# A hand-written order of tasks on five engines: the start of a modulated attention and gated block in another order, the values of tile 3 first

## The chip, the cores and the metric

The kernel runs on one core of a Trainium2 chip. The metric is the device time of one execution in microseconds. Beside the runs that only give a time there is one profiled execution, whose trace gives the start and length of every instruction.

## What is computed

The input `x` has 2048 rows of 512 (bf16). A vector `c` gives six rows of modulation. The first half is a linear attention of 32 heads of 16, whose features are two softmaxes; the second half is a gated block with 1376 hidden columns.

```python
mod = (silu(c) @ w_mod).reshape(1, 6, 1, -1)        # sa, ca, ga, sb, cb, gb
h = layernorm(x) * (1 + ca) + sa
q, k, v = split_heads(h @ wqkv)                      # 32 heads of 16
phi(t) = concat(softmax(t @ w_phi), softmax(-(t @ w_phi)))
kv = sum_s phi(k)_s v_s ;  z = sum_s phi(k)_s
o = phi(q) kv / (phi(q) z + 1e-6)
x = x + ga * (o @ wo)
h = layernorm(x) * (1 + cb) + sb
return x + gb * ((sigmoid(h @ w_gate) * (h @ w_up)) @ w_down)
```

## The kernel before

The 2048 rows are 16 tiles of 128. Everything is cut into 1230 named tasks, each a few instructions on one engine, and a text, `ORDER` (from line 39), lists them all. `arrange` (line 137 on) goes through the text word by word. It gives each task its engine (the first one the task allows, or the one behind `@`: A is ScalarE, D is VectorE, P is GpSimd) and gives each buffer a slot at its first use; a slot goes back to the end of its free list when the last user in the text is past. `emit` then issues the tasks in that order. So the text sets three things: the order of each engine's queue, the engine of some tasks, and which buffer a task takes over from which. An engine works its queue strictly in order; a task whose input is missing holds up all that stands behind it on the same engine. PSUM is eight banks, handed on in this way.

The names that are needed here, with their lines:

- `ld_*` (lines 533 to 563): loads, issued by SyncE onto one queue. `ld_x0b` is tiles 2 and 3 of x, `ld_x0a` tiles 0 and 1, `ld_wk0`/`ld_wk1` the key weights, `ld_wm00a` to `ld_wm01b` four quarters of the modulation weights (256 KB each, line 542), `ld_x3a` tiles 12 to 15 of x (512 KB, line 537), `ld_wv0` all value weights (512 KB, line 551), `ld_wmga` the modulation weights for ga (512 KB, line 555). `wqT*` are transposing loads of the query weights (line 669).
- `warm0`, `warm1_0` to `warm1_11` (line 600): matmuls on zeros, which nothing reads.
- `c1`, `c2`, `c3`: silu of c. `modc1.0`, `modc1.1` (line 630): the products that give sa and ca, the first for columns j = 0, 1, the second for j = 2, 3; `modc1c0`, `modc1c1` copy them out.
- `tpw*`, `wTc*`, `fold1*`, `foldc1*` (lines 661 to 685): key weights transposed, multiplied with w_phi, copied; `fold0*` the same for the queries.
- `st1_t` (lines 702, 703): statistics of tile t on VectorE. `rs1_g` (line 709 on ScalarE, 712 on GpSimd): the inverse deviation of group g; groups are tile 0, tile 1, tiles 2 and 3, and so on in pairs. `nmr1_g` (718), `xn1_t` (727 ScalarE, 729 VectorE, 731 GpSimd): the normalised tile.
- `tphgj` (line 744): TensorE transposes column block j of group g into a bank. `hm1_gj` (751 ScalarE, 753 VectorE): modulation of that block, out of the bank into `h1T`.
- `Kt`, `Vt`, `Qt` (lines 817, 821, 871): four matmuls of 512 columns each. For tiles 0 to 7 K, and for tiles 0 to 3 V, are halves: `K3a` takes j = 0, 1, `K3b` j = 2, 3. `K3a` needs `hm1_20`, `hm1_21` and the folded key weights; `V3a` needs `hm1_20`, `hm1_21` and `ld_wv0`.
- `et`, `nt`, `rt`, `phit` (776 to 798): exponentials on ScalarE, sums and reciprocals mainly on VectorE, the features. `vat` copies V out on ScalarE, `kvt` accumulates phi(k) v.
- `num`, `rd`, `u`, `out`, `x1`, `st2`, `xn2`, `mod`: the rest of the attention and the second norm. `gk.f`, `uk.f`, `tgk.f`, `hmk.f`, `yt.f` (lines 447, 457, 468, 485): the gated block of chunk k; chunk 0 is tile 0, chunk 1 is tile 1, then come 2, 4, 4 and 4 tiles. `g1.2` is the first gate product of the second chunk.

A load also waits for an earlier load: eight semaphores go round among the transfers.

## Time and profile before

| | us |
|---|---|
| three runs | 202.90, 204.34, 409.55 (median 204.34) |
| profiled execution | 203.25 |
| its span, first to last instruction | 201.3 |
| TensorE busy | 193.6 |
| VectorE busy | 160.0 |
| ScalarE busy | 104.9 |
| GpSimd busy | 103.9 |

How to read the profile. PE is TensorE's matmuls, PEld its weight loads, DVE is VectorE, ACT ScalarE, POOL GpSimd, SP SyncE. `L817` is line 817 of the kernel. A row of the timeline gives start, length, engine, line, operation, what it writes and reads, and how many were merged (`x6`); in square brackets stands the idle time before it and what ended it. A row of the waits gives who waited for whom, the total, how often and the longest. A row that ends in `KB, 5.0` is an issued transfer with its size and its time from issue to landing.

### The profile page before, as it was taken

How to read it: one execution, taken by the hardware profiler on the slowest of the kernel's cores; microseconds unless marked ns; L12 is line 12 of the kernel's file. 1: busy time of each engine (PE TensorE's matmuls, PEld its weight loads, DVE VectorE, ACT ScalarE, POOL GpSimd, SP SyncE). 2: the span in 40 equal slices, each digit the busy share in tenths (PEclk: the TensorE clock that was granted, in tenths of full speed). 3: DMA queues.
4: the chain of work that ended last, by engine and by line, in shares of the span. 5: the costliest groups of instructions: out<-in, count | busy, mean ns of one | idle time of the engine just before them, and what ended most of it. 6: DMA issues, size and time to landing. Idle time of an engine off the chain costs nothing.

```text
span 201.3 us, 4128 instructions
## 1 busy us (share of the span) xinstructions
PE 193.6 (96%) x1447; PEld 106.1 (53%) x1471; DVE 160.0 (79%) x376; ACT 104.9 (52%) x250; POOL 103.9 (52%) x146
## 2 busy tenths in 40 slices
PE   7889999999999999999999999999999999999993
PEld 2555665455565777668744444444444444444442
DVE  3999999999999999997997796875969662326632
ACT  2899999999978974486621215312112420334100
POOL 4889978887899998876660166130030332000000
PEclk9999999999999999999999999999999999999999
DMA  5999956729964883455573334442113031000011
GB/s 163 336 292 236 295 204 126 113 62 268 396 248 78 133 111 68 85 34 105 104 80 80 70 62 102 84 110 56 25 25 74 2 78 55 26 8 26 28 55 55
DMA packets 49453, 22.94 MB, mean 114 GB/s; under 512 B 38065, under 2 KB 47634, under 8 KB 49426
## 3 DMA queue, kind: packets, MB, share of 16 engines
q1 hardware_dynamic: 48896, 22.59, 48.8%
q8 instruction: 13, 0.21, 0.4%
q14 instruction: 14, 0.11, 0.2%
q10 hardware_dynamic: 530, 0.02, 0.1%
HBM read 11.58 MB, written 2.10 MB: 68 GB/s over the span
## 4 chain that ended last, share of the span: by engine, by line
PE 64%; DVE 26%; issue 5%; ACT 2%; DMA 1%; DVEq 0%
PE y_ps L485 19%; PE u_ps L447 18%; PE g_ps L447 18%; DVE ks L780 6%; PE a_ps L356 5%; DVE st L702 5%; DVE qks L780 3%; DVE phi L787 3%; DVE kr L798 2%; PE num L326 2%; DVE h1T L753 2%; DMA x_sb<-in_A_x_dram 1%; DVE mv L703 1%; PE g_ps L449 1%; DVE nmr L718 1%
## 5 line engine op out<-in xcount | busy, mean ns | idle before, releaser
L457 ACT ACTIVATE tg<-g_ps 128x512 bf16<-128x512 f32 (+5 forms) x66 | 28.7, 455 | 66.6 <-PE g_ps L447 39.7
L468 DVE SCALAR_TENSOR_TENSOR wmod_sb<-tg,u_ps 128x512 bf16<-128x512 bf16 (+4 forms) x63 | 30.2, 491 | 18.1 <-ACT tg L457 11.5
L485 PE MATMUL y_ps<-wd_sb,wmod_sb 128*128 128x512 bf16 (+4 forms) x180 | 44.2, 366 | 0.2
L447 PEld LDWEIGHTS <-wg_sb 128*128 128x128 bf16 (+1 forms) x252 | 21.9, 99 | 16.1 <-issue 0.2
L447 PEld LDWEIGHTS <-wu_sb 128*128 128x128 bf16 (+1 forms) x252 | 21.7, 99 | 15.9 <-issue 0.2
L784 POOL TENSOR_TENSOR qphi<-qe,qks 128x512 bf16<-128x512 bf16 x24 | 25.2, 1066 | 3.9 <-DMA pT<-qphi 1.6
L485 PEld LDWEIGHTS <-wmod_sb 128*128 128x128 bf16 (+1 forms) x187 | 17.1, 98 | 16.0 <-issue 0.6
L447 PE MATMUL u_ps<-wT_sb,wu_sb 128*128 128x512 bf16 (+2 forms) x124 | 23.8, 322 | 0.1
L447 PE MATMUL g_ps<-wT_sb,wg_sb 128*128 128x512 bf16 (+2 forms) x122 | 23.0, 321 | 0.2
L447 PE MATMUL g_ps<-wqk_sb,wg_sb 128*128 128x128 bf16 (+4 forms) x127 | 19.9, 286 | 0.1
L447 PE MATMUL u_ps<-wqk_sb,wu_sb 128*128 128x128 bf16 (+4 forms) x127 | 19.8, 286 | 0.1
L492 DVE TENSOR_TENSOR ot<-y_ps,x 128x512 bf16<-128x512 f32 (+2 forms) x17 | 11.1, 654 | 10.4 <-PE y_ps L485 10.3
L780 DVE TENSOR_REDUCE ks<-e 128x64 f32<-128x1024 bf16 (+2 forms) x22 | 19.2, 901 | 0.0
L780 DVE TENSOR_REDUCE qks<-qe 128x64 bf16<-128x1024 bf16 x16 | 19.1, 1202 | 0.0
L376 POOL TENSOR_SCALAR ve<-mv 128x2 f32<-128x2 f32 (+1 forms) x8 | 1.8, 225 | 33.3 <-DVE mv L366 33.2
L776 ACT ACTIVATE e<-k_ps 128x512 bf16<-128x512 f32 (+2 forms) x44 | 18.2, 519 | 0.0
L776 ACT ACTIVATE qe<-q_ps 128x512 bf16<-128x512 f32 x32 | 17.0, 611 | 0.8 <-POOL phi L787 0.5
L817 PE MATMUL k_ps<-wqk_f,h1T 128*128 128x512 bf16 x61 | 16.0, 379 | 0.1
L787 POOL TENSOR_TENSOR phi<-e,kr 128x1024 bf16<-128x1024 bf16 (+2 forms) x10 | 14.8, 1484 | 2.6 <-DVE phi L787 1.2
L356 PE MATMUL a_ps<-wo_sb,oT 128*128 128x512 bf16 x60 | 15.9, 379 | 0.2
L871 PE MATMUL q_ps<-wqk_f,h1T 128*128 128x512 bf16 x61 | 15.7, 379 | 0.1
L821 PE MATMUL v_ps<-wv_sb,h1T 128*128 128x512 bf16 x61 | 15.4, 379 | 0.1
(132 smaller groups left out, 305.6 us busy)
## 6 DMA issues: line engine op xcount, KB each, us to landing
out_dram<-ot SPq DMA_DIRECT2D x15, 128.0 KB, 1.7
x_sb<-in_A_x_dram SPq DMA_DIRECT2D x6, 256.0 KB, 4.7
wmod_sb<-in_w_mod_dram SPq DMA_DIRECT2D x1, 1536.0 KB, 7.0
wu_sb<-in_B_w_up_dram SPq DMA_DIRECT2D x1, 1376.0 KB, 11.5
wg_sb<-in_B_w_gate_dram SPq DMA_DIRECT2D x1, 1376.0 KB, 11.9
wd_sb<-in_B_w_down_dram SPq DMA_DIRECT2D x1, 1280.0 KB, 8.5
wmod_sb<-in_w_mod_dram SPq DMA_DIRECT2D x4, 256.0 KB, 6.1
wqk_sb<-in_A_wqkv_dram SPq DMA_DIRECT2D x2, 256.0 KB, 4.4
```

The costliest lines, as they stand in the source:

```text
L356: pe.matmul(ap_[:], lhsT=oT[:, j, :], rhs=wo_sb[:, j, :], start=(j == 0), stop=(j == KT - 1))
L447: pe.matmul(ps[:fsz, 0:n], lhsT=w[:, j, ft * P:ft * P + fsz], rhs=h[:, j, 0:n], start=(j == 0), stop=(j == KT - 1))
L457: G.add(f"tg{k}.{ft}", {"ACT": 0.13 + n * 0.00083}, lambda e, tg=tg, g_ps=g_ps, fsz=fsz, n=n: act.activation(tg[:fsz, 0:n], g_ps[:fsz, 0:n ...
L468: dve.scalar_tensor_tensor(hm_all[:fsz, hm[k].slot, ft, 0:n], tg[:fsz, 0:n], 1.0, u_ps[:fsz, 0:n], op0=ALU.add, op1=ALU.mult)
L485: mm = pe.matmul(y[:, 0:c1 - c0], lhsT=hm_all[:fsz, hm[k].slot, ft, tl * P:(tl + 1) * P], rhs=wd_sb[:fsz, ft, c0:c1], start=(ft == 0), sto ...
L776: act.activation(ee[:, a:b, s].rearrange("p g f h -> p g (f h)"), kp[:, a * 64:b * 64].rearrange("p (g n) -> p g n", n=64), ACT.Exp, scale ...
L780: dve.tensor_reduce(ks[:, a:b].rearrange("p g s h -> p (g s) h"), ee[:, a:b].rearrange("p g s f h -> p (g s) h f"), axis=AX.X, op=ALU.add)
L784: engine(e).tensor_tensor(ph[:].rearrange("p (g s f h) -> p g s f h", s=2, f=DH, h=4)[:, :, s], ee[:, :, s], ks[:, :, 1 - s].unsqueeze(2). ...
L787: engine(e).tensor_tensor(ph[:, a * P:b * P].rearrange("p (g f h) -> p g f h", f=DH, h=4), ee[:, a:b].rearrange("p g s f h -> p (g s) f h" ...
L817: pe.matmul(kp[:], lhsT=h1T[:, j, t * P:(t + 1) * P], rhs=wqk_f[:, j, D:2 * D], start=(j == 0), stop=(j == KT - 1))
L821: pe.matmul(vp[:], lhsT=h1T[:, j, t * P:(t + 1) * P], rhs=wv_sb[:, j, :], start=(j == 0), stop=(j == KT - 1))
L871: pe.matmul(qp[:], lhsT=h1T[:, j, t * P:(t + 1) * P], rhs=wqk_f[:, j, 0:D], start=(j == 0), stop=(j == KT - 1))
```

## The change

Only the text `ORDER` changes, and in it only the first 582 words, up to `g1.2`; the 648 words from there on are the same in both, and so are all tasks and what they need from each other. SyncE's queue keeps its order up to `ld_wo`, its 23rd entry. Three tasks go to another engine: `rs1_0` from GpSimd to ScalarE, `rs1_1` and `xn1_3` from ScalarE to GpSimd.

On TensorE the queue around the beginning is, before: ... `modc1.0 warm1_10 tph11 tph12 warm1_11 tph01 tph23 fold13 tph00 modc1.1 K3a tph02 tph03 K0a tph41 tph40 K2a fold01 tph42 K2b K0b K3b tph32 tph30 tph31 tph33 K1a K1b V0a` ..., and after: ... `tph21 warm1_9 tph20 modc1.0 warm1_10 tph22 warm1_11 tph03 fold13 tph11 tph23 modc1.1 tph10 V3a tph12 K3a tph13 fold01 tph40 tph41 tph42 V3b K0a tph30 tph33 tph32 K3b tph31 K0b tph43 K2a K2b K1a V1a K1b V2a` ... . On VectorE, `st1_0` and `xn1_0` come five and six places earlier, `hm1_10` five later, `st1_9` behind `hm1_40` and not ahead of it. On ScalarE the queue behind `modc1c0` is now `hm1_01 hm1_00 hm1_20 hm1_11 hm1_21 foldc13 hm1_22 hm1_12 hm1_03 foldc01 hm1_13 hm1_42 va3`. Later on, most tasks move by zero to five places on their engine, a few by more (`V6` 17 earlier, `V12` 12, `Q5` 10).

The beginning of the diff, where this stands:

```diff
-wdz warm0 c1 warm1_0 warm1_1 warm1_2 warm1_3 warm1_4 warm1_5 warm1_6 warm1_7 ld_x0b pmem ld_x0a ld_wk0 tpw1 tpw0 bd c2 mask4 st1_3 st1_2 st1_1 ld_x1b warm1_8
-rs1_2 rs1_1 nmr1_2 ld_wk1 xn1_3@A c3 wTc1 ld_x1a warm1_9 xn1_2 tph22 tph20 tpw2 tph21 wTc0 nmr1_1 st1_6 wTc2 xn1_1 tph13 ld_wm00b st1_0 tph10 tpw3 wTc3 fold10
-rs1_0@P fold12 st1_7 foldc10 ld_wm00a foldc12 fold11 modc1.0 rs1_4@P ld_x2b warm1_10 foldc11 modc1c0 st1_5 tph11 tph12 ld_wm01b warm1_11 st1_4 rs1_3@P
-hm1_20@A xn1_0 hm1_10 hm1_11@A hm1_21@A tph01 tph23 fold13 tph00 nmr1_4 xn1_6 xn1_7 ld_wm01a st1_11 hm1_01@A foldc13 st1_10 modc1.1 K3a modc1c1@D ld_x2a
-hm1_00@A tph02 hm1_23 rs1_6@P hm1_13@A hm1_02 nmr1_3 st1_9 st1_8 xn1_5 tph03 K0a tph41 hm1_03@A tph40 xn1_4 K2a hm1_22@A hm1_12@A hm1_41@A hm1_40 wqT1 nmr1_6
-ld_x3a st1_15 fold01 foldc01 tph42 K2b hm1_42@A K0b K3b e0.0 ld_wv0 tph32 tph30 tph31 wqT3 tph33 rs1_5@P nmr1_5 K1a hm1_32 xn1_11 hm1_30@A st1_14 n0.0 st1_12
-xn1_10 xn1_9 K1b e2.0 e3.0 rs1_8@P V0a wqT2 xn1_8 hm1_31@A tph43 V2a V2b nmr1_8 xn1_15 xn1_14 ld_wmga wqT0 V3a V3b va3 V0b fold03 V1a modca.0 modca.1 hm1_33
-tph50 V1b e1.0 K5a n2.0 r0.0@A modcac hm1_50 n3.0 hm1_43@A foldc03 xT1_11 fold02 fold00 foldc02 phi0.0 tph52 foldc00 xT1_10 va2 va1 n1.0 va0 K5b K4a r3.0
-st1_13 tph53 hm1_63@P hm1_60@P K4b hm1_62@P Q0 hm1_53@A tph51 Q1 ld_wmm2 tph82 hm1_51@A r2.0@A Q2 r1.0 phi3.0@D phi1.0@D hm1_82@A qe0.0 Q4 modc2.0 phi2.0@D
...
+wdz warm0 c1 mask4 pmem ld_x0b warm1_0 warm1_1 warm1_2 warm1_3 warm1_4 st1_3 warm1_5 ld_x0a st1_2 bd ld_wk0 c2 tpw0 rs1_2 st1_0 rs1_0 tpw1 wTc0 ld_x1b st1_1
+rs1_1@P warm1_6 nmr1_2 ld_wk1 wTc1 warm1_7 tpw2 xn1_3 xn1_0 tph02 tph00 ld_x1a st1_6 wTc2 tpw3 ld_wm00b fold10 warm1_8 nmr1_1 xn1_2 fold11 fold12 tph01 wTc3
+tph21 st1_7 c3 warm1_9 ld_wm00a foldc10 ld_x2b tph20 foldc11 foldc12 modc1.0 xn1_1 warm1_10 tph22 warm1_11 st1_4 rs1_4@P st1_5 modc1c0 hm1_01@A hm1_00@A tph03
+st1_10 ld_wm01b nmr1_4 ld_wm01a fold13 rs1_3@P tph11 tph23 hm1_20@A hm1_11@A modc1.1 st1_11 ld_x2a tph10 xn1_7 wqT1 hm1_21@A nmr1_3 modc1c1@D foldc13 hm1_10
+hm1_22@A ld_x3a hm1_02 ld_wv0 V3a tph12 wqT3 K3a xn1_6 hm1_12@A hm1_23 tph13 fold01 tph40 xn1_5 hm1_03@A tph41 tph42 foldc01 xn1_4 st1_8 hm1_13@A hm1_40 V3b
+K0a tph30 st1_9 rs1_6@P rs1_5@P tph33 st1_15 wqT2 hm1_42@A va3 hm1_41@A tph32 ld_wmga K3b tph31 nmr1_6 xn1_11 hm1_31@A st1_14 K0b tph43 hm1_30@A e3.0 e0.0 K2a
+K2b hm1_32 nmr1_5 xn1_10 hm1_43@A K1a V1a st1_12 wqT0 n3.0 K1b rs1_8@P V2a nmr1_8 V1b fold03 n0.0 V2b e1.0 V0a modca.0 e2.0 modca.1 xn1_8 xn1_9 xn1_15 tph50
+V0b xn1_14 modcac r0.0@A phi0.0 hm1_33 tph51 fold02 hm1_50 xT1_11 va2 va0 tph53 K5a n1.0 xT1_10 r3.0 st1_13 hm1_63@P hm1_60@P foldc02 hm1_62@P K5b hm1_53@A
+fold00 rs1_7@P va1 K4a tph52 foldc00 foldc03 n2.0 r1.0 ld_wmm2 K4b phi3.0@D V6 tph82 phi1.0@D tph80 hm1_51@A hm1_80@A Q0 r2.0@A phi2.0@D nmr1_7 ld_wo qe0.0
...
```

## The prediction, made before the changed kernel ran

> **What bounds the kernel now.** I read the page first, then busy time by stretch, then the timeline of single engines around the reordered part. The profiled execution took 203.25 us with a span of 201.3, so 1.95 us lie outside the span. The table by stretch (columns: busy time of PE, PEld, DVE, ACT and POOL, clock, DMA share, GB/s) shows where idle time is left:

> ```profile
> span 201.3 us, 4128 instructions
> PE 193.6 (96%) x1447; PEld 106.1 (53%) x1471; DVE 160.0 (79%) x376; ACT 104.9 (52%) x250; POOL 103.9 (52%) x146
> ...
> 5.00:13.00 8.00, 6.85 (x89) 4.28 (x88) 7.65 (x27) 7.30 (x19) 6.55 (x12) 1.00 1.15 311
> 13.00:17.00 4.00, 3.95 (x39) 2.44 (x37) 3.86 (x15) 4.00 (x11) 3.83 (x7) 1.00 1.13 324
> 17.00:66.00 49.00, 48.11 (x439) 26.67 (x446) 48.79 (x102) 46.51 (x121) 43.59 (x46) 1.00 0.76 197
> 66.00:92.00 26.00, 25.75 (x295) 19.41 (x297) 24.74 (x75) 17.25 (x48) 22.37 (x27) 1.00 0.58 81
> 92.00:198.00 106.00, 105.17 (x587) 52.02 (x596) 72.88 (x157) 28.35 (x52) 25.17 (x38) 1.00 0.29 61
> ```

> From 13 us to 198 TensorE is idle for 0.05 + 0.89 + 0.25 + 0.83 = 2.0 us of 185. Busy time alone would not prove that it is full, since matmuls overlap, but their spacing does: eight 512-column matmuls take 1.73 us in the chain of waits, 0.216 each, whereas an early one takes about twice that (below).

> ```profile
> 75.07 1.73 PE a_ps L356 x8
> ```

> So from 13 us on TensorE's queue is one gapless string: whatever it waits there is not made up later. VectorE, too, is full to 66 us (48.79 of 49 in its row) and ScalarE nearly (46.51), so no engine has room to hurry. The only loose stretch is before 13 us. What ends the waits there is a transfer: both halves of the modulation product wait for w_mod.

> ```profile
> 10.08 0.55 PE L630 MATMUL modc_ps<-sc_bf,wmod_sb 128*128 128x1 bf16 x16 [0.35 <-DMA wmod_sb<-in_w_mod_dram]
> ...
> 12.58 0.55 PE L630 MATMUL modc_ps<-sc_bf,wmod_sb 128*128 128x1 bf16 x16 [0.46 <-DMA wmod_sb<-in_w_mod_dram]
> 12.99 0.38 PE L817 MATMUL k_ps<-wqk_f,h1T 128*128 128x512 bf16 x1
> 13.42 0.27 PE L744 MATMUL tp_h<-ident,xn 128*128 128x128 bf16 x2
> ...
> 14.98 1.46 PE L817 MATMUL k_ps<-wqk_f,h1T 128*128 128x512 bf16 x6
> 16.27 0.61 PE L744 MATMUL tp_h<-ident,xn 128*128 128x128 bf16 x8
> 16.72 1.03 PE L817 MATMUL k_ps<-wqk_f,h1T 128*128 128x512 bf16 x4
> 17.59 0.59 PE L821 MATMUL v_ps<-wv_sb,h1T 128*128 128x512 bf16 x2
> ```

> The reader is to see that the gapless string starts with K3a at 12.99 (keys, L817), and that the first product with the value weights, V0a (L821), comes only at 17.59.

> **The change part by part.** No task is added or removed; the order of each queue is new up to g1.2.

> *The loads.* SyncE's first 23 entries keep their order, and the first 19, all loads, wait for no engine; so w_mod arrives as before, modc1.1 runs again at 12.58 and TensorE is free at 13.1, whatever was shuffled ahead of it. The shuffling before that (tph02 and tph00 first, tph21 and tph20 later) is costed at nothing: it is hidden by the two waits for w_mod, 0.35 and 0.46 us. Without that cover it would be worth at most the 8.00 - 6.85 = 1.15 us that TensorE idles from 5 to 13.

> *Three tasks change engine.* rs1_0 goes from POOL to ACT, rs1_1 and xn1_3 from ACT to POOL. The scaling xn1_3 costs 0.80 us on ACT and half of 1.52 on POOL:

> ```profile
> 6.57 0.80 ACT L727 ACTIVATE xn<-x_sb,nmr,rs 128x512 bf16<-128x512 bf16 x1
> 6.35 1.52 POOL L731 TENSOR_SCALAR xn<-x_sb,rs,nmr 128x512 bf16<-128x512 bf16 x2
> 8.61 0.24 POOL L712 TENSOR_SCALAR ve<-mv 128x1 f32<-128x1 f32 x1 [0.74 <-DVE mv L703]
> 8.94 0.58 POOL L713 TENSOR_TENSOR rs<-ve,mhalf 128x1 f32<-128x1 f32 x1
> ```

> POOL's queue now is rs1_1 (0.9 with its gap, from about 6.9), xn1_3, xn1_2, xn1_1 (0.77 each): they end near 8.6, 9.4 and 10.1. tph21, which needs the first two, is reached by TensorE near 9, so it waits some 0.4 us, still ahead of w_mod at 10.08. Cost nothing; uncovered, 0.4.

> *Values of tile 3 first.* This is the edit that decides. Behind modc1.1 and tph10 TensorE now has V3a, ahead of K3a, tph12, tph13, fold01, tph40 and all later work. V3a needs the whole load of the value weights, and that load stands where it stood:

> ```profile
> 10.22 0.57 SPq L537 DMA_DIRECT2D x_sb<-in_A_x_dram  x1
> 10.84 0.51 SPq L551 DMA_DIRECT2D wv_sb<-in_A_wqkv_dram  x1
> ...
> 14.38 0.58 SPq L555 DMA_DIRECT2D wqk_sb<-in_w_mod_dram  x1
> ...
> x_sb<-in_A_x_dram SPq DMA_DIRECT2D x1, 512.0 KB, 5.0
> wqk_sb<-in_w_mod_dram SPq DMA_DIRECT2D x1, 512.0 KB, 6.4
> 13.50:15.20 1.70, 1.70 (x18) 1.09 (x18) 1.67 (x7) 1.70 (x5) 1.62 (x4) 1.00 1.06 336
> 15.20:16.70 1.50, 1.50 (x14) 0.91 (x13) 1.47 (x6) 1.50 (x4) 1.42 (x4) 1.00 1.19 330
> ```

> No row gives its landing, so I bound it. The 512 KB of x ahead of it on the same queue are issued at 10.22 and land 5.0 later, at 15.2. The 512 KB behind it land at 14.38 + 6.4 = 20.8, and the old kernel used the weights at 17.59. So 15.2 to 17.6. Between: 524 kB at 330 GB/s are 1.6 us behind 15.2, so **16.8**. V3a, ready to go at 13.1, waits 3.7 us, and TensorE's queue stands still behind it.

> *The sum.* What TensorE has to do from V3a on in the new order is what it had to do from K3a on in the old one: of the tasks ahead only tph12 and tph13 went behind, and tph02 and tph03 came ahead, four transposes of one size. So the string that began at 12.99 begins at 16.8: +3.8 us. From that I take back some of the 2.0 us of idle time in the string, those waits which end on another engine that lags less. The rows:

> ```profile
> PE num L326 <- DVE kvb L294: 0.3, 1, 0.3
> PE kvacc L282 <- POOL phi L787: 0.2, 1, 0.2
> ...
> 14.21 0.68 DVE L702 BATCH_NORM_STATS2 st<-x_sb 128x6 f32<-128x512 bf16 x1
> 15.03 0.66 DVE L702 BATCH_NORM_STATS2 st<-x_sb 128x6 f32<-128x512 bf16 x1
> ...
> 15.82 0.38 DVE L753 TENSOR_SCALAR h1T<-tp_h,modc 128x256 bf16<-128x256 bf16 x1
> ...
> 13.00 2.46 ACT L751 ACTIVATE h1T<-tp_h,modc 128x128 bf16<-128x128 bf16 x6
> ```

> VectorE's hm1_40 (15.82 here) needs tph40, now behind V3a, tph12, K3a, tph13 and fold01: 16.8 + 0.43 + 0.06 + 0.43 + 0.06 + 0.22 = 18.0, with its own 0.11 and the way out about 18.3. That is 2.5 late, and st1_9 (one step of 0.8, from 14.21 to 15.03) is still to do: lag 3.3. ScalarE's hm1_12, the fifth of six from 13.00 at 0.4 each, so 14.6, starts near 17.5 with hm1_13 and hm1_03 still to do: lag 2.9 + 0.8 = 3.7. VectorE lags 0.5 less than TensorE, and only waits of about 0.5 us end on it or on POOL, so I take 0.2 back: +3.6. Made against the profiled execution: **203.25 + 3.6 = 206.9**. That execution lies 1.09 below the 204.34 shown as the median of three runs, whose lowest is 202.9; against that median the forecast is +1.2%, against its own execution +1.8%.

> *The rest of the order, 17 to 77 us.* Many neighbours swap (V6 17 places earlier, kv and reciprocals by a few). At most the 0.89 + 0.25 = 1.1 us that TensorE idles from 17 to 92 can be won, and a swap that runs into a busy bank could lose as much. I take zero: the sets of tasks are the same and VectorE has no gap to fill.

> [...] TensorE starts slow here: six matmuls take 2.74 us, about 0.43 apart, and the pair at 6.54 is 0.21 apart. The eight of the second group take 0.3 us more than at that rate, so the slow rate ends about half a microsecond into it, near 4.7.

> ```profile
> 1.25 2.74 PE L600 MATMUL warm<-wd_sb 128*128 128x512 bf16 x6 [1.25 <-DVE wd_sb L593]
> ...
> 4.11 2.15 PE L600 MATMUL warm<-wd_sb 128*128 128x512 bf16 x8
> ...
> 6.54 0.59 PE L600 MATMUL warm<-wd_sb 128*128 128x512 bf16 x2
> ```

> A pause of 3.7 us could bring that back; the profile of before has no pause near that length, so no row bears on it. [...]

> **The rivals.**
> - *The pause also slows TensorE.* Once slow, it works at half rate for about as long as at the start, 1.25 to about 4.7, 3.5 us, and loses half: +1.7, up to 3.5 if it takes twice as long. 206.9 + 1.7 = 208.6, up to 210.4. For it: the start. Against: modc1.1 and tph10 run at 12.6 to 13.2, so the empty stretch is only just as long as the start-up. Chance 0.2.
> - *ScalarE holds TensorE up after the pause.* Eight banks pass between them, and tph33, K2a and V2a each take a bank that ScalarE empties, with hm1_13, hm1_41 and e3.0. ScalarE lags 3.7 and was full; three waits of about 0.4 give +1.2: 208.1. Against: lags of 3.7 and 3.8 are nearly equal. Chance 0.12.
> - *Not slower: the value weights are there in time.* The landing is worked out, not seen. If they landed by 13.1, V3a would start where K3a did: 203.3, or, with the idle time from 17 to 92 won, 202.2. Each microsecond of landing after 13.1 costs one. Against: x, ahead on the same queue, landed at 15.2. This is also the case in which the change just reorders. Chance 0.08.

> **How the numbers follow.** The forecast, the pause alone, has 0.6, and reaches from 15.2 to 17.6 in the landing: 203.25 + 2.2 to 203.25 + 4.6, so 205.4 to 207.9 with 206.9 likeliest. The range reaches to the slow-rate case: 204.6 to 209.2, leaving out the not-slower case and that rival's upper part. Over 2% slower, about what a measurement here can tell from no change, begins at 207.3 from the profiled execution and at 208.4 from the median: most of the slow-rate case and half of the bank case, 0.2, and a quarter of the forecast, 0.15, give 0.35. Over 2% faster has no mechanism: 0.02. The rest, 0.63, lies within 2%.

> **What would show it.** Right: L821 appears on TensorE ahead of L817, at 16.5 to 17, with 3.3 to 4 us idle before it, released by the load of wv_sb; L753 on VectorE idles 2.5 to 3.1 us near 15; ScalarE idles about 3 near 14; from 17 on everything is the old profile shifted. The slow rate would show as matmuls 0.43 apart behind the pause. Wrong: the first L821 at 13 to 14, or the pause there and the end not moved, which would mean that TensorE's string had slack.

## The result, and the profile after

The changed kernel took 209.31 us (median of five runs, 208.64 to 210.62) against 204.34 for the kernel before (five runs; one took 409.55 and is left out of the comparison). The ratio is 1.0282, 95% interval 1.0245 to 1.032: slower by 2.8%. The forecast was 206.9, its range ended at 209.2.

The page of the profiled execution (209.15 us) comes first. The row `PEclk` is the granted clock in 40 slices of 5.2 us, in tenths, 9 meaning full.

```profile
span 207.2 us, 4128 instructions
...
PE 195.7 (94%) x1447; PEld 107.3 (52%) x1471; DVE 160.6 (78%) x376; ACT 104.7 (51%) x249; POOL 105.0 (51%) x147
...
PEclk9995999999999999999999999999999999999998
...
L821 PE MATMUL v_ps<-wv_sb,h1T 128*128 128x512 bf16 x61 | 16.4, 391 | 3.7 <-DMA wv_sb<-in_A_wqkv_dram 3.6
```

The span grew by 5.9 us. The work is the same 1447 matmuls, yet TensorE is busy 2.1 us longer (195.7 against 193.6): they did not only wait, some ran slower. The fourth slice, 15.5 to 20.7 us, has the clock at half. The last row names the wait: the first product with the value weights stood 3.6 us for their load.

TensorE's timeline around it, to be read beside the one of before:

```profile
12.73 0.55 PE L630 MATMUL modc_ps<-sc_bf,wmod_sb 128*128 128x1 bf16 x16 [0.46 <-DMA wmod_sb<-in_w_mod_dram]
...
17.01 0.61 PE L821 MATMUL v_ps<-wv_sb,h1T 128*128 128x512 bf16 x1 [3.64 <-DMA wv_sb<-in_A_wqkv_dram]
...
17.94 1.06 PE L817 MATMUL k_ps<-wqk_f,h1T 128*128 128x512 bf16 x2
...
23.13 1.46 PE L817 MATMUL k_ps<-wqk_f,h1T 128*128 128x512 bf16 x6
```

`modc1.1` runs at 12.73, as good as before, and then TensorE stands until 17.01. The string that began with `K3a` at 12.99 begins with `V3a` 4.0 us later. Behind it two key products take 1.06 us, where the pair of matmuls at 6.54 in the kernel before took 0.59; from 23 on six take 1.46, as the six at 14.98 did before.

Busy time by stretch, columns as in the prediction, shows the same around the pause:

```profile
13.40:15.00 1.60, 0.00 (x0) 0.00 (x0) 1.56 (x6) 0.76 (x2) 1.60 (x3) 0.97 1.10 329
15.00:17.00 2.00, 0.00 (x0) 0.00 (x0) 0.14 (x1) 0.00 (x0) 1.36 (x3) 0.50 1.18 330
17.00:19.00 2.00, 1.77 (x6) 0.90 (x8) 0.00 (x0) 0.81 (x2) 0.00 (x0) 0.50 1.50 112
19.00:22.00 3.00, 3.00 (x22) 1.90 (x20) 2.14 (x8) 2.33 (x5) 0.81 (x2) 0.54 0.60 169
22.00:24.00 2.00, 2.00 (x17) 1.05 (x15) 1.95 (x7) 1.33 (x4) 1.83 (x4) 1.00 0.02 4
```

The clock column falls at the end of the first row and is back in the last one. The records of the granted clock in this trace have it at 0.5 from 14.91 to 21.74, 6.83 us. So the clock fell while TensorE was standing (1.5 us after it had stopped), and 4.73 us of work, 17.01 to 21.74, ran at half rate: half of that, an estimated 2.4 us, is lost on top of the wait.

What else waited between 13 and 198 us, from TensorE's waits:

```profile
PE v_ps L821 <- DMA wv_sb<-in_A_wqkv_dram: 3.6, 1, 3.6
PE num L326 <- DVE kvb L294: 0.4, 1, 0.4
PE tp_h L744 <- issue: 0.2, 1, 0.2
```

The second row was 0.3 before. The third is new; it stands at 17.84, inside the spell of half clock. A wait of 0.2 of `kvacc` for GpSimd is gone. The delay is complete when the gated block begins, and it stays. First the group of its gate products, kernel before (the first starts at 66.8) and after (73.0); then the same copy of VectorE near the end, before and after:

```profile
L447 PE MATMUL g_ps<-wqk_sb,wg_sb x127: 216/272/379, 66.8 to 160.0; 128*128 128x128 bf16 x40, 128*128 128x256 bf16 x40, 128*128 128x512 bf16 x39, 128*96 128x128 bf16 x4
```

```profile
L447 PE MATMUL g_ps<-wqk_sb,wg_sb x127: 218/272/379, 73.0 to 166.2; 128*128 128x128 bf16 x40, 128*128 128x256 bf16 x40, 128*128 128x512 bf16 x39, 128*96 128x128 bf16 x4
```

```profile
196.09 0.69 DVE L492 TENSOR_TENSOR ot<-y_ps,x 128x512 bf16<-128x512 f32 x1 [1.74 <-PE y_ps L485]
```

```profile
202.26 0.69 DVE L492 TENSOR_TENSOR ot<-y_ps,x 128x512 bf16<-128x512 f32 x1 [1.74 <-PE y_ps L485]
```

6.2 us late at 67 us and 6.2 us late at 196. The start gives 4.0 + 2.4 = 6.4; the 0.2 between is as much as the wait of `kvacc` that is gone.

### The profile page after: what moved, and what is told of

Read it like the earlier page. It is cut to its first block, busy times and chain, and to the rows that moved or that the text cites. A ratio compares the mean times of both kernels' runs of the same rounds, so it can differ in the third digit from the quotient of the medians.

```text
span 207.2 us, 4128 instructions
## 1 busy us (share of the span) xinstructions
PE 195.7 (94%) x1447; PEld 107.3 (52%) x1471; DVE 160.6 (78%) x376; ACT 104.7 (51%) x249; POOL 105.0 (51%) x147
## 4 chain that ended last, share of the span: by engine, by line
PE 69%; ACT 13%; DMA 5%; SPq 5%; DVE 4%; issue 3%; ACTq 0%; DVEq 0%
PE y_ps L485 18%; PE u_ps L447 17%; PE g_ps L447 17%; ACT e L776 6%; PE a_ps L356 6%; PE q_ps L871 4%; DMA wv_sb<-in_A_wqkv_dram 3%; PE num L326 2%; ACT vaug L836 2%; ACT h1T L751 2%; SPq L537 2%; DMA oT<-o 2%; SPq L542 2%; ACT qe L776 1%; PE g_ps L449 1%
## 5 line engine op out<-in xcount | busy, mean ns | idle before, releaser
L485 PE MATMUL y_ps<-wd_sb,wmod_sb 128*128 128x512 bf16 (+3 forms) x179 | 44.0, 366 | 0.2
L468 DVE SCALAR_TENSOR_TENSOR wmod_sb<-tg,u_ps 128x512 bf16<-128x512 bf16 (+4 forms) x63 | 30.3, 492 | 17.7 <-ACT tg L457 11.5
L821 PE MATMUL v_ps<-wv_sb,h1T 128*128 128x512 bf16 x61 | 16.4, 391 | 3.7 <-DMA wv_sb<-in_A_wqkv_dram 3.6
L817 PE MATMUL k_ps<-wqk_f,h1T 128*128 128x512 bf16 x62 | 17.2, 395 | 0.1
L787 POOL TENSOR_TENSOR phi<-e,kr 128x1024 bf16<-128x1024 bf16 (+2 forms) x10 | 14.7, 1481 | 3.4 <-ACT kr L795 1.8
L356 PE MATMUL a_ps<-wo_sb,oT 128*128 128x512 bf16 x61 | 15.8, 379 | 0.1
```

The costliest lines, as they stand in the source:

```text
L356: pe.matmul(ap_[:], lhsT=oT[:, j, :], rhs=wo_sb[:, j, :], start=(j == 0), stop=(j == KT - 1))
L468: dve.scalar_tensor_tensor(hm_all[:fsz, hm[k].slot, ft, 0:n], tg[:fsz, 0:n], 1.0, u_ps[:fsz, 0:n], op0=ALU.add, op1=ALU.mult)
L485: mm = pe.matmul(y[:, 0:c1 - c0], lhsT=hm_all[:fsz, hm[k].slot, ft, tl * P:(tl + 1) * P], rhs=wd_sb[:fsz, ft, c0:c1], start=(ft == 0), sto ...
L787: engine(e).tensor_tensor(ph[:, a * P:b * P].rearrange("p (g f h) -> p g f h", f=DH, h=4), ee[:, a:b].rearrange("p g s f h -> p (g s) f h" ...
L817: pe.matmul(kp[:], lhsT=h1T[:, j, t * P:(t + 1) * P], rhs=wqk_f[:, j, D:2 * D], start=(j == 0), stop=(j == KT - 1))
L821: pe.matmul(vp[:], lhsT=h1T[:, j, t * P:(t + 1) * P], rhs=wv_sb[:, j, :], start=(j == 0), stop=(j == KT - 1))
```

## The experiments

The theory after reading these profiles: `V3a` ahead of `K3a` makes the whole loss; it consists of the wait for the load and of a spell of half clock that follows. What sets the clock was a second question: the length of the pause, or the share of work in fixed stretches of 3.41 us. In the clock records of this trace the spells last 10.24 us at full rate, 6.83 at half, 184.32 at full and 3.41 at half, which is 3, 2, 54 and 1 times 3.413. The runs were made in three groups, each on one chip and beside the kernel before: `e1` to `e4` (kernel before 203.72), `e5` to `e8` (204.72), `e9` to `e11` (204.76). Between groups the ratios are compared, not the times.

**One task alone: `e2_v3a_alone`.** The kernel before, with only `V3a` put first. The loads keep their order; four words of SyncE's queue are written earlier so that the load is ahead of the task in the text.

```diff
 ... st1_10 modc1.1
-K3a modc1c1@D ld_x2a
+ld_x2a wqT1 ld_x3a ld_wv0 V3a K3a modc1c1@D
...
-... wqT0 V3a V3b va3 ...
+... wqT0 V3b va3 ...
```

> The order of before, with V3a alone taken ahead of K3a (the loads keep their order). Theory: one task moved is enough for the whole loss: L821 first at 16.9 behind 3.7 us of waiting, granted clock 0.5 for about 7 us, time 209 to 210. Rival (the loss needs the new order as a whole): within 1 us of before, or at most the wait of 3.7, 207.

209.82 us (209.06 to 210.54), ratio 1.0297 (1.0247 to 1.0348). The row of its timeline:

```profile
17.20 1.03 PE L821 MATMUL v_ps<-wv_sb,h1T 128*128 128x512 bf16 x2 [3.73 <-DMA wv_sb<-in_A_wqkv_dram]
```

The clock was at 0.5 from 14.69 to 21.52, and all four runs have a mean clock of 0.983 or 0.984. One task out of the 582 that were reordered makes the whole loss.

**The reverse: `e1_v3_back`.** The changed kernel with `V3a` and `V3b` behind `V1b`, and `va3` ahead of `va2`.

```diff
-tph10 V3a tph12 K3a ... tph42 V3b K0a ... V1b fold03
+tph10 tph12 K3a ... tph42 K0a ... V1b V3a V3b fold03
```

> V3a, V3b and va3 go back behind V1b; all the rest of the new order stays. Theory (the early product with the value weights makes TensorE wait 3.7 us for their load, and the wait also slows TensorE's clock for some 2.3 us more): both go, L821 starts near 18 with no wait on the load, the granted clock stays 1.00, and the time is that of the kernel before, 203.3 to 204.3. Rival (the rest of the new order costs, by the handing on of banks between TensorE and ScalarE or by GpSimd's three more tasks): 205 or more, with waits of TensorE on ScalarE between 13 and 60 us.

205.07 us (204.43 to 207.31), ratio 1.005 (1.0011 to 1.0089). In its timeline the keys are first again, and the values come at 19.74 without a wait:

```profile
13.89 0.93 PE L817 MATMUL k_ps<-wqk_f,h1T 128*128 128x512 bf16 x2
...
19.74 0.59 PE L821 MATMUL v_ps<-wv_sb,h1T 128*128 128x512 bf16 x2
```

So the rest of the new order costs about 1 us (0.2 to 1.8 by the interval) where the prediction had taken zero (with bounds of 1.1 either way) and 203.3 to 204.3 was expected of this run. In this profile `modc1.1` waits 0.47 us for ScalarE and runs at 13.09. The profiled run itself was the slowest, 207.31, with a clock of 0.5 from 14.01 to 17.42 though TensorE paused for no more than half a us; that was the first sign against the length of the pause.

**The load earlier: `e4_wv_first`.** The changed kernel; on SyncE the value weights go ahead of tiles 8 and 9 of x, of the first transposing load and of tiles 12 to 15.

```diff
-ld_wm01a ld_x2a wqT1 ld_x3a ld_wv0
+ld_wm01a ld_wv0 ld_x2a wqT1 ld_x3a
```

> The changed kernel, with the load of the value weights issued ahead of tiles 8 and 9 of x, the first transposing load and tiles 12 to 15 of x. Theory: it lands near 14.3 (512 KB at 330 GB/s behind w_mod at 12.6), V3a waits about 1.1 us, the clock holds, and VectorE waits a few tenths for the tiles of x behind it: 204.5 to 205.5. If the clock falls even so, about 207. Rival (the load's place does not matter): 209.

207.22 us (205.15 to 208.47), ratio 1.0189 (1.0132 to 1.0247). The wait shrinks from 3.64 to 0.84:

```profile
14.03 0.60 PE L821 MATMUL v_ps<-wv_sb,h1T 128*128 128x512 bf16 x2 [0.84 <-DMA wv_sb<-in_A_wqkv_dram]
```

The four runs fall apart by their clock. The one at 1.00 took 205.15; those at 0.98, 0.98 and 0.988 took 208.47, 207.89 and 206.56. One kernel in one order thus shows a second price beside the wait, 1.4 to 3.3 us, that goes with the clock. (Only the first of the four has a timeline.)

**Work in the pause: `e3_fill16`.** The changed kernel with sixteen matmuls on zeros ahead of `V3a` (their result is used nowhere), so that TensorE streams while the load is on its way.

```diff
+    warm("warm2", 16, 3.46, r=["c1"], w=["warm"])
...
-tph10 V3a
+tph10 warm2 V3a
```

> The changed kernel, with 16 more matmuls on zeros (3.5 us at 0.216) between tph10 and V3a, whose result nothing reads. V3a still starts when the value weights land, at 17.0. Theory: the clock does not drop, so only the wait is left: granted clock 1.00, time 203.3 + 3.8 = 207.0, some 2.2 less than the changed kernel. Rival (the part above 3.8 us comes from elsewhere, such as banks or ScalarE): no gain from the filling, 209 as the changed kernel.

209.37 us (208.21 to 211.3), ratio 1.0282 (1.0202 to 1.0362), where 207.0 was expected. The clock did what the theory says (the seventh column; of the four runs one had 0.99, the others 1.00):

```profile
13.00:17.00 4.00, 3.87 (x31) 1.72 (x27) 2.12 (x9) 1.14 (x3) 3.32 (x6) 1.00 1.09 316
17.00:21.70 4.70, 4.68 (x38) 2.81 (x39) 3.05 (x10) 3.98 (x10) 1.66 (x3) 1.00 1.01 158
```

and `K15` ran at 44.02 instead of 45.93. But `kv8.0` was at 53.70, hardly ahead of 53.81 in the changed kernel. In between stand these two, from VectorE's and from GpSimd's timeline:

```profile
47.50 2.42 DVE L788 TENSOR_TENSOR phi<-e,kr 128x1024 bf16<-128x1024 bf16 x1
```

```profile
47.46 1.91 POOL L788 TENSOR_TENSOR phi<-e,kr 128x1024 bf16<-128x1024 bf16 x1 [0.34 <-PE kvacc L282]
```

`phi7.0` on VectorE took 2.42 us; in the changed kernel it takes 0.72. It began 0.04 us behind `phi9.0` on GpSimd and ended 0.55 behind it. TensorE then stood 1.83 us for it, which is most of what the clock had gained:

```profile
49.98 0.43 PE L282 MATMUL kvacc<-vaug,phi 128*128 128x68 bf16 x8 [1.83 <-DVE phi L788]
```

**The same without the collision: `e5_fill16_swap`, `e9_fill8_swap`.** `e5` is `e3` with `phi7.0` one normalisation earlier on VectorE (and `e11.6` behind `r7.0` on ScalarE, so that it can start); `e9` is `e5` with eight matmuls on zeros and not sixteen.

```diff
-n8.0 r7.0@A ... V9 n11.6 K14 e11.4 e11.0 phi7.0@D r8.0
+n8.0 r7.0@A e11.6 ... V9 phi7.0@D n11.6 K14 e11.4 e11.0 r8.0
```

> The run with 16 filling matmuls ahead of V3a, and on VectorE phi7.0 one place earlier, ahead of n11.6 (on ScalarE e11.6 one place later, behind r7.0, so that phi7.0 can start). There phi7.0 took 2.42 us on VectorE, having started 0.04 us behind phi9.0 on GpSimd, which ran 1.91; in the other runs it takes 0.72. [...] Rival (the half rate was worth nothing, since VectorE's lag of the wait sets the end anyway): 209.4 as without the swap.

> The run with filling and with phi7.0 one place earlier, with 8 filling matmuls in place of 16: TensorE works to about 14.9 and then stands still to 17.0. In the profiles so far the clock fell after each stretch of 3.41 us in which matmuls streamed for 13 to 35% of it, and held after those with 39% and more. Theory (the clock goes by the share of work in fixed stretches, with a limit between 35 and 39%): the stretch with the pause has some 40% or more for most positions, so the clock holds in most runs and the time is that with 16, 3.3 us over before. Rival (it goes by the length of the pause, of which 2.1 us are enough, as one of 2.8 was): clock 0.98 to 0.99 in all runs, 4.5 to 6 us over before.

`e5`: 207.99 us (207.85 to 209.04), where 207.0 to 207.9 was expected; ratio 1.0156 (1.0087 to 1.0225), the clock at 1.00 in every run. `phi7.0` is short now and GpSimd loses little (two in 4.02, where two of 1.91 would be 3.82):

```profile
46.87 0.68 DVE L788 TENSOR_TENSOR phi<-e,kr 128x1024 bf16<-128x1024 bf16 x1
```

```profile
47.18 4.02 POOL L788 TENSOR_TENSOR phi<-e,kr 128x1024 bf16<-128x1024 bf16 x2 [0.34 <-PE kvacc L282]
```

`e9`: 207.32 us (206.9 to 207.67), ratio 1.0127 (1.0082 to 1.0172). Its stretches:

```profile
13.40:15.00 1.60, 1.55 (x7) 0.58 (x6) 1.56 (x6) 0.73 (x2) 1.60 (x3) 1.00 1.04 326
15.00:17.00 2.00, 0.34 (x2) 0.11 (x2) 0.05 (x1) 0.00 (x0) 1.34 (x3) 1.00 1.19 321
17.00:19.00 2.00, 2.00 (x20) 1.28 (x19) 0.69 (x2) 1.52 (x4) 0.00 (x0) 1.00 1.39 99
```

```profile
16.79 0.60 PE L822 MATMUL v_ps<-wv_sb,h1T 128*128 128x512 bf16 x2 [1.66 <-DMA wv_sb<-in_A_wqkv_dram]
```

TensorE stands for 1.66 us, up to 16.79, and the clock does not fall. What is left with the clock held is the wait (and the rest of the order): 1.27% and 1.56% of 204.7, 2.6 and 3.2 us.

Both kernels hold two edits, the filling and the moved `phi7.0`. What the filling gives can be read ahead of the move, at the first product that goes into `kvacc` (line 282 of the changed kernel): it starts at 35.34 in the changed kernel, at 33.22 in `e3`, 32.94 in `e5` and 32.99 in `e9`, so 2.1 to 2.4 us earlier.

**The changed kernel beside it: `e11_changed_again`.** No edit.

> The changed kernel itself, beside the two others on the same chip. Theory: the wait and the half rate together, 5.5 to 6 us over before, clock 0.98 in all runs, and 2 to 2.6 us over the run with 8 filling matmuls. Rival (the difference to the filled runs was one of chips): under 1 us over it.

210.0 us (209.02 to 210.96), ratio 1.0238 (1.019 to 1.0286), 2.7 us over `e9` on the same chip (2.3 by the ratios); the clock is 0.984 in two runs, 0.990 and 0.992 in the others, where 0.98 in all was expected:

```profile
15.00:17.00 2.00, 0.00 (x0) 0.00 (x0) 0.15 (x1) 0.00 (x0) 1.43 (x3) 0.70 1.34 265
17.00:19.00 2.00, 1.51 (x4) 0.69 (x6) 0.00 (x0) 0.55 (x2) 0.00 (x0) 0.50 1.44 80
19.00:22.00 3.00, 3.00 (x17) 1.84 (x16) 1.88 (x6) 2.33 (x6) 0.54 (x2) 0.50 0.75 209
```

The same half rate. In this profile the load is there half a us later than in `e9` (`V3a` at 17.27, not 16.79), so not all of the difference need be the clock's.

**A shorter pause at the same place: `e8_pause2`.** The kernel before with one matmul ahead of `K3a` that reads tile 12 of x, whose load lands earlier than the value weights.

```diff
+        pe.matmul(ps[:], lhsT=x_sb[:, 12, 0:P], rhs=wd_sb[:, FT - 1, :], start=True, stop=True)
...
-modc1.1 K3a modc1c1@D ld_x2a
+modc1.1 ld_x2a wqT1 ld_x3a pause K3a modc1c1@D
```

> The order of before, with one more matmul ahead of K3a that reads tile 12 of x and whose result nothing reads; tiles 12 to 15 land at 15.2. So TensorE pauses for 2.2 us at 13.0, and nothing else is moved. Theory: the end moves by the pause if the clock holds, 205.4 to 205.8; where the clock falls, by up to 2.4 more, 207 to 208. Rival (a pause of this length is absorbed, as VectorE has its own queue): under 204.5.

208.32 us (207.13 to 209.04), ratio 1.017 (1.0105 to 1.0236), the clock at 0.984 to 0.992 in all runs. Timeline and stretches of the profiled one (207.13):

```profile
15.59 0.61 PE L607 MATMUL pause<-wd_sb,x_sb 128*128 128x512 bf16 x1 [2.22 <-DMA x_sb<-in_A_x_dram]
15.99 0.63 PE L822 MATMUL k_ps<-wqk_f,h1T 128*128 128x512 bf16 x1
```

```profile
15.00:16.00 1.00, 0.41 (x2) 0.14 (x3) 0.00 (x0) 0.00 (x0) 0.00 (x0) 0.50 1.10 349
16.00:18.40 2.40, 2.18 (x11) 1.30 (x11) 1.19 (x4) 1.10 (x3) 0.51 (x1) 0.50 1.55 179
18.40:20.00 1.60, 1.60 (x14) 0.90 (x12) 1.55 (x7) 1.39 (x4) 1.44 (x4) 1.00 0.89 255
```

With 2.22 us of standing the clock fell here, and with 1.66 in `e9` it did not. The keys start 3.0 us late and then run at half rate from 15.99 to 18.41, which is worth 1.2: together 4.2, and the last copy of this execution is 4.2 us later than in the kernel before.

**Less work and no pause: `e7_less_warm`.** The kernel before without the last four single matmuls on zeros between the transposes.

```diff
-    for i in range(12):
+    for i in range(8):
```

> The order of before without the matmuls on zeros warm1_8 to warm1_11 (4 of 12; nothing reads them). No wait is added. Theory (the clock follows how much TensorE works in a stretch of 3.4 us, not whether it stands still): the stretch from 8.1 to 11.5 holds too little work, the granted clock is 0.5 for 3.4 or 6.8 us, of which 1.9 to 5.3 fall on the gapless string from 13 us on, and the time goes up by 1 to 2.6: 204.3 to 206. [...]

205.49 us (203.79 to 206.61), ratio 1.0008 (0.9966 to 1.005): the same time. But the mean clock was at or below 0.992 in eight of ten runs, and the profiled one, in which TensorE pauses for no more than 0.6 us around the fall, has it at 0.5 from 11.86 to 15.27:

```profile
8.40:11.90 3.50, 2.31 (x38) 1.54 (x36) 3.36 (x12) 3.31 (x9) 2.26 (x6) 0.99 1.17 308
11.90:13.30 1.40, 1.25 (x20) 0.98 (x19) 1.36 (x4) 1.40 (x4) 1.40 (x3) 0.50 1.50 161
13.30:15.30 2.00, 1.78 (x16) 0.90 (x14) 1.55 (x8) 1.57 (x5) 1.53 (x4) 0.51 1.03 307
```

The clock falls without a pause, as expected; that it would cost 1 to 2.6 us was wrong. 1.4 of the 3.4 us at half rate lie ahead of 13.3, where TensorE still has some slack, and four matmuls are saved; that this makes up for the rest was not tested.

**More work in the kernel before: `e10_before_fill`.** Two matmuls on zeros ahead of each half of the modulation product.

```diff
-fold11 modc1.0 ... st1_10 modc1.1 K3a
+fold11 warm2_0 modc1.0 ... st1_10 warm2_1 modc1.1 K3a
```

> The order of before with two more matmuls on zeros ahead of modc1.0 and two ahead of modc1.1, where TensorE waits 0.51 and 0.62 us for w_mod. Theory (what the runs of before that show a clock of 0.99 lose is the same fall of the clock, from a stretch with too little work): clock 1.00 in all runs, none of them 1.5 us over the others, median 0.2 to 0.5 under before. Rival (those runs are slow for another reason): as many runs at 0.99 as before, same median. If the filling is in the way of the products behind it: 0.2 to 0.4 slower.

204.83 us (203.58 to 207.13), ratio 0.9984 (0.9953 to 1.0015). The clock was 1.00 in all twelve runs (0.997 the lowest), where 6 of 16 runs of the kernel before on this chip had 0.99. Those six have a median of 205.8 us, the other ten 204.5, so one spell of half rate goes with some 1.2 us there. One run of `e10` took 207.13 us at a clock of 1.00, so the clock isn't the only cause of long runs. The edit brings nothing that can be measured; the filling takes some of it back, since it waits 0.24 us for ScalarE to empty a bank, and the product comes at 13.39, where the kernel before has it at 12.58:

```profile
12.96 0.59 PE L600 MATMUL warm<-wd_sb 128*128 128x512 bf16 x2 [0.24 <-ACT h1T L753]
13.39 0.54 PE L632 MATMUL modc_ps<-sc_bf,wmod_sb 128*128 128x1 bf16 x16
```

In this profile TensorE also stands 1.08 us at 56.92 for a `phi` of VectorE that began 0.09 us behind one on GpSimd and took 1.53.

No version is measurably faster than the kernel before.

**The collision alone: `e6_collide`.** The kernel before with `phi7.0` two places later on VectorE.

```diff
-n11.6 phi7.0@D n11.0 K10 n14.0 n11.2
+n11.6 n11.0 K10 n14.0 phi7.0@D n11.2
```

> The order of before, with phi7.0 on VectorE two places later, behind n11.0 and n14.0, so that it starts some 0.6 us after phi9.0 on GpSimd. [...] Rival (TensorE has enough to do and VectorE's lag is absorbed): within 0.4 of before.

205.25 us (204.58 to 207.34), where 204.3 to 205.0 was expected; ratio 1.0033 (0.9997 to 1.0069). VectorE's row, then GpSimd's:

```profile
44.39 1.80 DVE L787 TENSOR_TENSOR phi<-e,kr 128x1024 bf16<-128x1024 bf16 x1
```

```profile
43.73 1.91 POOL L787 TENSOR_TENSOR phi<-e,kr 128x1024 bf16<-128x1024 bf16 x1 [0.31 <-DVE ks L780]
```

The stretching is shown again (1.80, where about 2.1 was expected), and TensorE stands 1.83 us for it (46.24), as in `e3`. Its price on the end is not shown: some 0.7 us, not clear of zero, less than the 0.8 to 1.4 expected. The medians of `e3` and `e5` are 1.4 us apart, but on two chips; by the ratios it is 1.3%, 2.6 us. In the profiles TensorE stands 1.83 us for a `phi` of VectorE in `e3` and 0.5 in `e5`, so the collision makes about 1.3 of it; what makes the rest stays open.

## Why the prediction was wrong

- **TensorE's gapless string; nothing made up later.** Right: 6.2 us late at 67 us, 6.2 at the end.
- **Loads as they were, `modc1.1` again at 12.58, early shuffling free.** Right to 0.15 us: 12.73.
- **The landing at 16.8, a wait of 3.7.** Right: 17.01 and 3.64. The first term of the sum, +3.8, measured +4.0 in the profile.
- **The lags.** ScalarE's `hm1_12` was put near 17.5, VectorE's `hm1_40` at 18.3. The timelines of the two show more, since what feeds them ran at half rate:

```profile
18.19 0.81 ACT L751 ACTIVATE h1T<-tp_h,modc 128x128 bf16<-128x128 bf16 x2 [4.03 <-PE tp_h L744]
```

```profile
19.79 0.41 DVE L753 TENSOR_SCALAR h1T<-tp_h,modc 128x256 bf16<-128x256 bf16 x1 [4.65 <-PE tp_h L744]
```

- **The rest of the order, zero.** `e1` has 0.5%, about 1 us, at the edge of the bounds, so this term was taken too small; `e2` reaches the whole loss without that order, so the two do not simply add.
- **The rival "ScalarE holds TensorE up".** Not seen: no wait of TensorE's matmuls behind the pause ends on ScalarE.
- **The step that failed** is the dismissal of the first rival, "the pause also slows TensorE". It had 0.2 and its 1.7 to 3.5 us were left out of the sum; the mean clock is 0.981 to 0.992 in all nine runs of the changed kernel, and the half rate costs 2.4 in the profile, 2.3 to 2.7 between `e11` and `e9`. Its price had been estimated rightly (208.6 to 210.4 around 209.3). What was wrong was the ground for the small chance: "modc1.1 and tph10 run at 12.6 to 13.2, so the empty stretch is only just as long as the start-up". That weighed the length of the pause against that of the slow start, and no row had shown that the clock goes by it. The runs do not order by length: `e9` stands for 1.7 us and keeps its clock, `e8` stands for 2.2 and loses it, `e7` and `e1` stand for no more than 0.6 and lose it; in the changed kernel the clock goes 1.5 us into the pause.

What fits all profiles is this reading. In the clock records of the kernel before the spell at full rate lasts 197.97 us, 58 times the same 3.413 that fits the changed kernel's spells 3, 2, 54 and 1 times. From the first rise of the clock to its fall it was 10.24 us in `after`, `e2`, `e8` and `e11` and 6.83 in `e1` and `e7`, three and two times 3.41. So I count stretches of 3.41 us from the first rise, and the changes in these records stand at their ends. Counting the columns that TensorE streamed in each stretch, at 0.216 us per 512 (0.43 at half rate, as the two key products from 17.94 to 18.80 have it), and taking the stretches with the least work, gives this estimate:

| share of the stretch | at its end |
|---|---|
| after 14%, `e2` 22%, `e1` 35%, `e7` 28%, `e8` 13%, `e11` 2% | clock fell to 0.5 |
| before 41%, `e4` 39%, `e5` 41%, `e6` 49%, `e9` 50, 49 and 55%, `e10` 47% | clock stayed |
| while at 0.5: after 27%, `e2` 27%, `e11` 45% | stayed at 0.5 |
| while at 0.5: `e7` 66%, `e8` 71%, `e1` about 100% | clock rose |

The earlier stretches of the kernels in the first row held at 41% or more. In the changed kernel the stretch that decided ended at 14.9 and held more than the pause: from 11.5 on TensorE mostly did sixteen one-column matmuls and transposes. The kernel before is itself at the edge (41%), which would explain why some of its runs have a clock of 0.99.

That the clock would fall in `e7` and hold in `e9` and `e10` was expected from such a share before they ran; the table was drawn up after the runs. How a matmul at the edge of a stretch is counted moves the shares of the first two rows by up to seven points, so the limit in these profiles is no sharper than between 30 and 40%. The profile's busy time of TensorE does not order them. The clock fell after the first of these two stretches (`e1`) and held after the second (`e9`), though TensorE (second column) was busy for less of it, with 35% and 55% by columns:

```profile
10.60:14.00 3.40, 2.77 (x47) 1.94 (x48) 3.02 (x12) 3.19 (x10) 2.85 (x5) 1.00 1.29 227
15.31:18.73 3.42, 1.95 (x18) 1.27 (x19) 0.42 (x2) 1.25 (x4) 1.03 (x3) 1.00 1.31 197
```

So of the two it is the columns that fit; what exactly is counted stays open. So does the exact split: wait and rest of the order 2.6 to 3.2 us, half rate 2.3 to 2.7, against 5.8 for the whole (2.82% of 204.34). The string starts 4.0 us late, and in the profiles the last copy of `e9` is 3.7 us later than that of the kernel before, but its median is only 2.6 over the kernel before beside it. Whether part of the wait is given back, or the kernel before loses something on that chip, was not followed up.

## What to carry to other kernels

Before a product is put first, look up when its own load lands: here 4 us of TensorE's queue stood behind one task, and the loads had not moved. Price a stall of a full TensorE twice, once for its length (here 4.0 us) and once for the half rate that may follow (here an estimated 2.4), and do not judge the second by the stall's length alone: 1.7 us of standing kept the clock in `e9`, 2.2 lost it in `e8` and 0.6 in `e7`. What ordered these profiles was the estimated share of columns streamed in the 3.41 us that decided, with thin matmuls and transposes counted by their columns: up to 35% lost the clock, 39% and more kept it. Filling the stall with matmuls on zeros kept the clock and saved that part of the loss (`e9` against `e11`, 2.3 to 2.7 us), but not the wait, and in `e3` the gain was lost again where VectorE's `phi` now ran into GpSimd's (2.42 us in place of 0.72). The wait itself shrank to 0.84 us with an earlier load (`e4`) and went with the product put back behind its load (`e1`).
